# H3 mixer with token MLP on one core: the table of the last inverse stage turned by DMA transposes instead of TensorE

## The chip, the cores and the metric

One Trainium2 chip, one of its cores. The metric is the device time of one execution in microseconds (us). Engines are called by the names of the profile: PE is the matrix engine (PEld its weight loads), ACT the scalar engine, DVE the vector engine, POOL the general engine, SP the engine that mainly issues transfers. SPq stands for instructions of SP's queue that issue transfers.

## What is computed

The reference, cut to what matters (S = 2048 tokens, D = 448 channels, F = 1792; all inputs bf16):

```
x  = A_q
kv = causal_conv4(A_k, A_shift_k) * A_v                    # 4 taps along the tokens
y  = irfft(rfft(kv, 2S) * rfft(A_ssm_k, 2S))[:S]           # long convolution along the tokens
h  = x + layernorm(x) * (y + kv * A_ssm_D)
n  = layernorm(layernorm(h))
h2 = h + (gelu(n^T w1 + b1) w2 + b2)^T                     # MLP along the tokens
```

## The kernel before

**Tiles.** One SBUF tensor ("arena" in the profile) holds everything at fixed byte offsets, one PSUM tensor ("ps") has eight banks. Tokens are split as 128 partitions times R = 16 rows, so a tile is 128 x 448 bf16 for each row r.

**Stages**, each a function that appends operations under a tag. `tables` builds the tables of sines and cosines: E (32 blocks of 128 x 128 in f16; the Sin activations are tables.6:3 and tables.5:3) and the small FW, MA, MB, MN. `kT` turns the filter, `kv` does the short convolution and the product with v. `k1`, `u1` (emit_stage1) are the first forward stage of the filter and of kv: matmuls with E at L1059, evacuations at L1069 (L1067 where the D term is added), shuffles between partitions by DMA at L1075. `k2`, `u2` (emit_stage2) are the second one (matmuls L1094, evacuations L738 to L742). `i1` (emit_products_i1) multiplies the two spectra on DVE (L1160), does the first inverse stage (matmuls L1177, evacuations L738) and shuffles into TZ (L1200; the last pair in four smaller transfers, L1189). `i2` (emit_i2) is the last inverse stage: row r is two matmuls (L1299) with the blocks 2r and 2r + 1 of **ET**. ET is E with each 128 x 128 block turned. Rows 0 and 1 (r < NZ = 2) take the last pair's part from TU through EW (four more matmuls each, L1307), a small copy of ET's first blocks (transfers L1127, ct0.1:2 to 5; zeros by L1118, ct0.1:0 and 1). Then come the gate (L1316), the products, the two layernorms (statistics of x in `q`: L1236; the normalized Q at L1385) and `mlp`: first layer from W1A (L1432, weight loads L1405 called w1a.0 to w1a.3) and W1B (L1442), gelu (L1422), second layer (L1453, L1456), stores. `warm` are 14 matmuls that nobody reads (L1210), `xload` loads x in four parts (L915), `xn` normalizes x rows 0 to 3 on ACT (L1269).

**ET before.** emit_ct (L1103) is called once from i1 for the first eight blocks (step ct0.0) and once later for the other 24 (steps ct.0, ct.1, ct.2). Each step is eight PE transposes into one PSUM bank and one copy to SBUF by ACT or DVE (L738, L741).

**What sets the order.** Each engine works through its queue in order. The queues are written out in ORDER, one string per engine: a token like `i1.4:9-15` is operations 9 to 15 of step i1.4. Operations that may run on ACT or DVE are placed by the string in which they stand. Dependencies come from the byte ranges that an operation reads and writes and from `after`; the program waits on semaphores for them. shuf["u"] is the list of u1's shuffles. In i1, steps run i1.1, i1.14, i1.8, i1.10, i1.12, i1.6, i1.4, i1.16 (pairs jj = 0, 6, 3, 4, 5, 2, 1, 7); operations 18 and up of a step are its shuffles. The last queue entries of ACT before i2 are

```
i1.4:8 i1.4:17 xn.1:0 xn.2:0 i1.16:18 i1.16:9 ct.2:8 ct.0:8 xn.5:0 xn.4:0 ct.1:8
```

and SP's from the end of u1 to the first weights

```
u1.15:11 xload.2:0 xload.0:0 ct0.1:1 ct0.1:0 w1a.0:0 xload.3:0 xload.1:0 ct0.1:5 ct0.1:2-4 i1.14:20 i1.1:20 i1.1:22 ...
```

Of the kernel before, what the change touches and what calls it, by code (L numbers as in the profile page):

```python
# [13 lines left out]
        "dummy.0:1-9 kv.4:0-11 kv.3:0-7 kv.6:0-11 kv.5:0-7 kT.0:0-7 kT.1:0-7 kT.1:9 kT.3:0-7 kT.2:0-7 kT.3:9 "  # L14
        "kT.5:0-7 kT.6:0-7 kT.7:0-7 kv.7:0-7 kT.5:9 bias.0:0 k1.8:0-7 k1.9:0-2 k1.12:0-7 k1.9:3-7 kv.1:0-7 "
        "kv.2:0-11 k1.13:0-7 k1.10:0-7 k1.11:0-7 kv.8:0-3 kT.4:0-7 kv.8:4-11 kv.10:0-23 kv.12:0-23 k1.14:0-7 "
        "kv.9:0-27 k1.15:0-7 k1.4:0-7 kv.11:0-27 u1.0:0-7 u1.1:0-7 k1.0:0-7 k1.1:0-7 u1.2:0-7 u1.3:0-7 kv.13:0-27 "
        "k1.5:0-7 kv.14:0-23 k1.6:0-7 u1.4:0-7 k1.2:0-7 u1.5:0-7 kv.15:0-27 u1.6:0-7 u1.7:0-7 k1.7:0-7 u1.8:0-7 "
        "k1.3:0-7 u1.9:0-7 k2.0:0-3 k2.1:0-3 k2.12:0-3 k2.13:0-3 k2.4:0-3 k2.5:0-3 kv.16:0-23 k2.9:0-3 k2.8:0-3 "
        "u1.10:0-7 u1.12:0-7 u1.13:0-7 u1.11:0-7 u1.14:0-7 u1.15:0-7 k2.2:0-3 k2.3:0-3 k2.7:0-3 k2.6:0-3 k2.10:0-3 "  # L20
        "k2.11:0-3 k2.14:0-3 k2.15:0-3 u2.0:0-3 u2.1:0-3 u2.12:0-3 u2.13:0-3 u2.8:0-3 u2.9:0-3 u2.6:0-1 u2.7:0-3 "
        "u2.6:2-3 i1.1:1-7 i1.1:10-17 i1.1:8 i1.14:10-16 i1.14:1-7 i1.14:17 i1.14:8 i1.8:1-7 i1.8:10-16 i1.8:8 "
        "i1.8:17 ct0.0:0-7 u2.10:0-3 u2.11:0-3 i1.10:1 i1.10:10-17 i1.10:2-8 u2.5:0-3 u2.4:0-3 i1.12:1-8 "
        "i1.12:10-17 u2.2:0-3 u2.3:0-3 u2.14:0-2 i1.6:1-8 i1.6:10-17 warm.13:0 u2.14:3 u2.15:0-3 i1.4:9-15 i1.4:0-7 "
        "i1.4:16 warm.9:0 warm.11:0 warm.5:0 warm.8:0 warm.1:0 i1.16:1-7 i1.16:10-16 i1.16:8 i1.16:17 warm.10:0 "
        "warm.4:0 warm.7:0 warm.6:0 warm.0:0 ct.2:0-7 warm.12:0 warm.3:0 ct.0:0-7 ct.1:0-6 warm.2:0 i2.1:0-1 "
        "i2.2:0-3 i2.9:0 ct.1:7 i2.9:1 i2.10:0-3 i2.28:0-1 i2.45:0-1 i2.17:0-1 i2.32:0-1 i2.20:0-1 i2.41:0-1 "
        "i2.54:0-1 mlp.0:1 mlp.0:4 mlp.0:2-3 mlp.0:6 mlp.0:5 i2.58:0-1 mlp.1:2 mlp.1:4 mlp.1:3 mlp.1:5 mlp.0:0 "
        "mlp.1:1 mlp.1:6 mlp.1:0 i2.67:0-1 mlp.2:2 mlp.2:4 mlp.2:6 mlp.2:5 mlp.2:1 mlp.2:0 mlp.2:3 i2.71:0-1 "
        "mlp.3:4-5 mlp.3:2-3 mlp.3:6 mlp.3:0-1 i2.80:0-1 mlp.4:1 mlp.4:3-4 mlp.4:2 mlp.4:5-6 mlp.4:0 i2.84:0-1 "  # L30
        "mlp.5:2-3 mlp.5:0-1 mlp.5:6 mlp.5:4-5 i2.93:0-1 mlp.6:3 mlp.6:1 mlp.6:4 mlp.6:6 mlp.6:0 mlp.6:5 mlp.6:2 "
        "mlp.7:6 mlp.7:5 mlp.7:0-1 mlp.7:3-4 mlp.7:2 i2.97:0-1 mlp.8:2 mlp.8:0 mlp.8:5 mlp.8:1 mlp.8:3-4 mlp.8:6 "
        "mlp.9:5-6 mlp.9:3 mlp.9:0 mlp.9:4 mlp.9:1-2 mlp.10:5 mlp.10:3 mlp.10:2 mlp.10:6 mlp.10:4 mlp.10:0-1 "
        "mlp.11:0 mlp.11:2 mlp.11:1 mlp.11:3 mlp.11:5 mlp.11:4 mlp.11:6 mlp.12:1 mlp.12:0 mlp.12:4 mlp.12:2 "
        "mlp.12:5-6 mlp.12:3 mlp.13:6 mlp.13:2 mlp.13:1 mlp.13:3 mlp.13:0 mlp.13:4-5 mlp.14:1 mlp.14:3 mlp.14:2 "
        "mlp.14:5 mlp.14:4 mlp.14:6 mlp.14:0 mlp.15:2-3 mlp.15:5 mlp.15:1 mlp.15:6 mlp.15:4 mlp.15:0 mlp.17:0-15 "
        "mlp.18:0-15 mlp.19:0-15 mlp.20:0-15 mlp.21:0-15 mlp.22:0-15 mlp.23:0-15 mlp.24:0-13 mlp.25:0-13 "
# [15 lines left out]
    "dve": (
        "dummy.0:0 tables.3:0-1 kv.0:3 tables.6:0 tables.4:16 tables.5:0 tables.4:17 tables.6:1 tables.4:18 "
        "tables.5:1 tables.4:19 tables.6:2 tables.4:20 kv.6:12 tables.5:2 kT.1:8 kT.3:8 tables.7:6 tables.7:4 "
        "kT.5:8 kT.6:8 tables.7:7 kT.7:8 kT.0:8 bias.0:1 kv.7:8 k1.12:8 kv.2:12 kv.0:4 kT.4:8 kv.8:12 kv.10:24-25 "
        "kv.12:25 kv.12:24 kv.9:28-29 kv.11:29 kv.11:28 k1.0:8 k1.1:8 kv.13:29 kv.13:28 kv.14:25 kv.14:24 k1.2:8 "
        "kv.15:28-29 u1.7:8 k1.3:8 k2.1:5 k2.5:4 kv.16:24-25 k2.9:5 u1.10:8 u1.11:8 k2.3:4 k2.7:4 bias.1:0 k2.11:4 "
        "k2.15:5 u2.1:5 i1.0:0 i1.1:0 i1.14:0 i1.13:0 i1.7:0 i1.8:0 i1.10:0 i1.9:0 ct0.0:8 q.1:0 q.1:2 q.1:1 q.1:3 "
        "i1.11:0 q.2:0 i1.12:0 q.2:1 u2.5:5 i1.5:0 i1.6:0 i1.3:0 q.2:2 i1.2:0 q.3:0 xn.0:1 q.2:3 i1.15:0 i1.16:0 "  # L60
        "q.4:0 q.4:2-3 q.4:1 q.3:1-3 q.5:0 q.5:2-3 q.5:1 q.6:2 q.6:0-1 xn.3:1 i2.3:0 q.6:3 i2.4:0 i2.11:0 i2.5:0 "
        "i2.12:0 i2.6:0 i2.13:0 i2.18:0 i2.14:0 i2.21:0 i2.8:0 i2.16:0 i2.30:0 i2.34:0 q.7:0 q.7:2 q.7:1 q.7:3 "
        "i2.26:0 q.8:0 q.8:2 q.8:1 q.8:3 i2.27:0 i2.43:0 i2.47:0 i2.39:0 i2.40:0 i2.60:0 i2.56:0 i2.69:0 i2.52:0 "
        "i2.53:0 i2.73:0 i2.94:0 i2.82:0 i2.65:0 i2.86:0 i2.98:0 i2.66:0 i2.78:0 i2.79:0 i2.99:0 i2.95:0 i2.92:0 "
        "i2.91:0 i2.104:0 i2.105:0 mlp.24:14 mlp.25:14 mlp.26:14 mlp.27:14 mlp.28:14 mlp.29:14 mlp.30:14 mlp.31:14 "
        "mlp.32:14 mlp.33:14 mlp.34:14 mlp.35:14 mlp.36:14 mlp.37:14 mlp.38:14 mlp.39:14 mlp.39:30 "
    ),
    "pool": (
        "tables.4:0 tables.4:2 tables.4:4 tables.4:6 tables.4:8 tables.4:10 tables.4:12 tables.4:14 tables.4:1 "
        "tables.4:3 tables.4:5 tables.4:7 tables.4:9 tables.4:11 tables.4:13 tables.4:15 tables.1:0 tables.0:1-2 "  # L70
        "tables.0:0 tables.0:3-4 loads.13:0 tables.2:0-1 tables.2:3 tables.2:5 tables.2:7-11 tables.2:2 tables.2:4 "
        "tables.2:6 q.0:0-1 kv.0:1-2 tables.7:0-3 tables.7:8-11 kv.0:0 k1.9:9-10 k1.13:9-10 k1.11:9-10 k1.15:9-10 "
        "u1.1:9-10 u1.3:9-10 k1.1:9-10 k1.5:9-10 u1.5:9-10 u1.7:9-10 k1.3:9-10 k1.7:9-10 u1.9:9-10 u1.13:9-10 "
        "u1.15:9-10 u1.11:9-10 ew.0:3 ew.0:1 ew.0:0 ew.0:2 i1.14:19 i1.14:21 i1.8:19 i1.8:21 q.1:4-5 i1.10:19 "
        "i1.1:19 xn.0:0 i1.12:19 i1.6:19-20 i1.4:18 i1.6:22 q.2:4 i1.16:21 q.2:5 xn.3:0 q.4:4-5 q.6:4-5 i2.7:0 "
        "i2.15:0 i2.23:0-2 i2.24:0 i2.25:0 i2.36:0-2 i2.37:0 i2.38:0 q.8:4-5 i2.49:0-2 i2.50:0 i2.51:0 i2.62:0-2 "
        "i2.63:0 i2.64:0 i2.75:0-2 i2.76:0 i2.77:0 i2.88:0-2 i2.89:0 i2.90:0 i2.0:0 i2.101:0-2 i2.102:0 i2.103:0 "
    ),
    "sp": (
        "loads.6:0 loads.8:0 loads.0:0 loads.1:0 loads.2:0 loads.3:0 loads.13:1 loads.14:0-1 loads.10:0 loads.5:0 "  # L80
        "loads.11:0 loads.4:0-2 loads.12:0 loads.7:0 loads.9:0 k1.11:11 k1.9:11 k1.13:11 k1.15:11 u1.1:11 k1.1:11 "
        "u1.3:11 k1.5:11 u1.7:11 k1.3:11 u1.5:11 u1.9:11 k1.7:11 u1.13:11 u1.11:11 u1.15:11 xload.2:0 xload.0:0 "
        "ct0.1:1 ct0.1:0 w1a.0:0 xload.3:0 xload.1:0 ct0.1:5 ct0.1:2-4 i1.14:20 i1.1:20 i1.1:22 i1.10:21 i1.1:21 "
# [499 lines left out]
def _build(nc, A_q, A_k, A_v, A_shift_k, A_ssm_k, A_ssm_D, B_w1, B_b1, B_w2, B_b2, out):  # L583
# [14 lines left out]
    f16 = DT.float16  # L598
# [917 lines left out]
```

## Time and profile before

| what | value |
|---|---|
| three runs, us | 172.63, 172.2, 175.94 (median 172.63) |
| span of the profiled execution, us | 171.2 |
| granted clock of PE | 1.000 |
| PE busy | 161.5 us, 94% |
| DVE, ACT, POOL busy | 99.1, 92.9, 58.1 us |
| DMA packets moved | 35.15 MB, mean 205 GB/s |

The profiled execution is one execution; its own figure is the span from the first to the last instruction, 171.2 us, and no other time of it is given. The runs above are separate executions. Busy shares are means over stages with different limits: PE is near full at the end and not in the middle. In the rows of a timeline the columns are start, us from the first to the last of the merged instructions, engine, line, operation, tiles, count, and in brackets the idle time before with what ended it.

### The profile page before, as it was taken

To read this page: it belongs to the slowest core of one execution; us is meant where nothing else is said; L and a number is where in the kernel's file an instruction comes from. 1 tells how busy PE (TensorE), PEld (TensorE's weight loads), DVE (VectorE), ACT (ScalarE), POOL (GpSimd) and SP (SyncE) were. 2 spreads that over 40 slices of the span, in tenths; PEclk is the share of its full clock that TensorE was granted. 3 is DMA by queue.
4 is the path that set the end of the run, shared out by engine and by line. 5 is a ranking of instruction groups with operands and counts; after the bars stand their busy time and mean duration, and the time that the engine had idled before them with its cause. 6 is when DMAs were issued, how large, how long until landed. Compare 5 with 4: busy or idle time off the path is not lost.

```text
span 171.2 us, 3572 instructions
## 1 busy us (share of the span) xinstructions
PE 161.5 (94%) x1425; PEld 94.7 (55%) x1425; DVE 99.1 (58%) x187; ACT 92.9 (54%) x133; POOL 58.1 (34%) x150
## 2 busy tenths in 40 slices
PE   6979999979889999988999999999999999999993
PEld 2765845443334434453555555555567777777783
DVE  7988988859899999969988810000003223132232
ACT  3798788988999999999877336321210000000000
POOL 8344827590820573466788820000000000000000
PEclk9999999999999999999999999999999999999999
DMA  5999587675749855667999999960000111101111
GB/s 156 417 315 386 176 257 280 230 301 193 255 120 369 302 173 175 206 182 237 344 342 405 415 419 425 414 279 0 0 0 4 54 54 54 54 4 54 54 54 54
DMA packets 15708, 35.15 MB, mean 205 GB/s; under 512 B 3564, under 2 KB 9980, under 8 KB 15692
## 3 DMA queue, kind: packets, MB, share of 16 engines
q1 hardware_dynamic: 13020, 29.20, 46.9%
q0 software_dynamic: 2528, 5.65, 10.2%
q8 instruction: 11, 0.18, 0.5%
q10 hardware_dynamic: 144, 0.08, 0.2%
q14 instruction: 5, 0.04, 0.1%
HBM read 22.05 MB, written 1.84 MB: 139 GB/s over the span
## 4 chain that ended last, share of the span: by engine, by line
PE 66%; ACT 14%; DMA 10%; DVE 4%; POOL 2%; SPq 2%; issue 1%; DVEq 0%
PE ps L1453 25%; PE ps L1432 12%; PE ps L1442 12%; ACT arena L738 7%; DMA arena<-arena 5%; DMA arena<-in_A_ssm_k_dram 5%; ACT arena L1069 4%; PE ps L1177 4%; PE ps L1094 3%; PE ps L1299 3%; POOL arena L1075 2%; PE ps L992 2%; PE ps L1059 2%; DVE arena L1007 2%; ACT arena L739 1%
## 5 line engine op out<-in xcount | busy, mean ns | idle before, releaser
L1456 DVE SCALAR_TENSOR_TENSOR arena<-ps,arena 128x448 bf16<-128x448 f32 (+2 forms) x17 | 11.2, 657 | 57.3 <-PE ps L1453 57.2
L1453 PE MATMUL ps<-arena 128*128 128x448 bf16 (+2 forms) x238 | 42.7, 342 | 0.0
L1453 PEld LDWEIGHTS ps<-arena 128*128 128x128 bf16 x238 | 33.3, 145 | 9.5
L738 ACT CAST arena<-ps 128x896 bf16<-128x896 f32 x30 | 24.6, 1012 | 0.2 <-PE ps L1094 0.2
L1432 PE MATMUL ps<-arena 128*128 128x448 bf16 x112 | 22.5, 353 | 0.6 <-DVE arena L1385 0.6
L1069 ACT CAST arena<-ps 128x896 bf16<-128x896 f32 x24 | 20.5, 915 | 3.9 <-PE ps L1059 3.8
L1075 POOL DMA_DIRECT2D arena<-arena x32 | 17.6, 554 | 12.2 <-ACT arena L1069 10.2
L1442 PE MATMUL ps<-arena 128*128 128x448 bf16 x112 | 21.3, 352 | 0.0
L1422 ACT ACTIVATE arena<-ps,arena 128x448 bf16<-128x448 f32 x14 | 8.2, 640 | 18.7 <-PE ps L1442 14.5
L1094 PE MATMUL ps<-arena 128*64 128x448 bf16 x128 | 15.2, 359 | 2.5 <-DMA arena<-arena 0.8
L1432 PEld LDWEIGHTS ps<-arena 128*128 128x128 bf16 x112 | 10.9, 98 | 11.1 <-DVE arena L1385 1.3
L1160 DVE TENSOR_TENSOR arena<-arena 128x1792 bf16<-128x1792 bf16 x16 | 16.7, 1086 | 0.3
L1442 PEld LDWEIGHTS ps<-arena 128*128 128x128 bf16 x112 | 11.0, 98 | 10.2
L1059 PE MATMUL ps<-arena 128*32 128x448 bf16 x256 | 15.0, 355 | 0.8 <-DVE arena L1007 0.5
L1177 PE MATMUL ps<-arena 64*128 64x448 bf16 x128 | 14.5, 351 | 0.1
L1094 PEld LDWEIGHTS ps<-arena 128*64 128x64 f16 x128 | 5.8, 108 | 10.9 <-ACT arena L738 2.9
L1200 POOL DMA_DIRECT2D arena<-arena x11 | 6.5, 593 | 15.3 <-ACT arena L738 15.3
L1177 PEld LDWEIGHTS ps<-arena 64*128 64x128 f16 x128 | 6.0, 94 | 8.3 <-ACT arena L738 2.5
L1007 DVE TENSOR_TENSOR arena<-ps,arena 128x512 bf16<-128x512 f32 (+1 forms) x16 | 9.1, 619 | 2.1 <-PE ps L992 1.8
L1355 ACT ACTIVATE arena<-arena 128x448 bf16<-128x448 bf16 x14 | 8.0, 572 | 3.7 <-DVE arena L1326 3.5
L738 ACT COPY arena<-ps 128x1024 bf16<-128x1024 bf16 (+1 forms) x8 | 8.0, 1067 | 3.0 <-PE ps L966 3.0
L1059 PEld LDWEIGHTS ps<-arena 128*32 128x32 f16 x256 | 5.1, 95 | 7.6 <-DVE arena L1007 2.5
(97 smaller groups left out, 192.5 us busy)
## 6 DMA issues: line engine op xcount, KB each, us to landing
arena<-in_B_w_dram SPq DMA_DIRECT2D x8, 896.0 KB, 8.7
arena<-in_B_w_dram SPq DMA_DIRECT2D x2, 2048.0 KB, 17.3
arena<-arena POOLq DMA_DIRECT2D x32, 112.0 KB, 3.2
arena<-arena SPq DMA_DIRECT2D x16, 224.0 KB, 3.2
arena<-in_B_w_dram SPq DMA_DIRECT2D x2, 1536.0 KB, 18.8
arena<-in_A_k_dram SPq DMA_DIRECT2D x4, 448.0 KB, 5.8
arena<-in_A_v_dram SPq DMA_DIRECT2D x4, 448.0 KB, 9.4
arena<-in_A_q_dram SPq DMA_DIRECT2D x4, 448.0 KB, 5.3
```

The lines of the kernel that those rows point to most:

```text
L738: return e.copy(out=dst(), in_=src())
L1007: return e.tensor_tensor(out=v, in0=u.rearrange("p t (r d) -> p t r d", d=64), in1=v, op=ALU.mult)
L1059: op("pe", lambda e, W, b=b, r=r, q=q, x=x, c0=c0: e.matmul(PS[32 * q:32 * q + 32, b.slots[x], 0:D], E[:, 2 * r + x, c0:c0 + 32], src[:, r ...
L1069: return e.copy(out=dst, in_=Ppair(b)) if W == "act" else e.tensor_copy(out=dst, in_=Ppair(b))
L1075: shuf[tag].append(op(q_, lambda e, W, g=g, i=i, a=a, nu=nu, jh=jh: e.dma_start(T[a + i:a + i + 4 * nu - 3:4].rearrange("p (j k) c d -> p ...
L1094: op("pe", lambda e, W, b=bs[h], h=h, j=j, c=c, par=par: e.matmul(PS[64 * par:64 * par + 64, b.slots[c], 0:D], FW[:, 64 * c:64 * c + 64], ...
L1160: op("dve", lambda e, W, m=m, i=i: e.tensor_tensor(out=MR(m.slots[0]).rearrange("p (x y) d -> p x y d", x=2), in0=TU[:, i].unsqueeze(2).br ...
L1177: k = op("pe", lambda e, W, b=bs[h], m=ms[h], par=par, t=t, tab=tab, xy=xy, P=P: e.matmul(Pb(b, par), tab[P, :], MR(m.slots[0])[P, xy, :], ...
L1432: op("pe", lambda e, W, r=r, fc=fc, b=bs[fc]: e.matmul(Pb(b), W1A[:, r, 128 * fc:128 * fc + 128], Q[:, r, :], start=(r == 0), stop=(r == R ...
L1442: op("pe", lambda e, W, r=r, fc=fc, b=b: e.matmul(Pb(b), W1B[:, r, 128 * (fc - n0):128 * (fc - n0) + 128], Q[:, r, :], start=(r == 0), sto ...
L1453: op("pe", lambda e, W, r=r, fc=fc, b=b, d0=d0, d1=d1: e.matmul(Pb(b)[:, d0:d1], W2[fc // 7][:, fc % 7, r:S:R], G[:, fc, d0:d1], start=(fc ...
L1456: op("dve", lambda e, W, r=r, b=b, d0=d0, d1=d1: e.scalar_tensor_tensor(out=X[:, r, d0:d1], in0=Pb(b)[:, d0:d1], scalar=bm[:, r:r + 1], in ...
```

## The change

emit_ct issues one DMA transpose from SBUF to SBUF per group of eight blocks, on SP, after u1's shuffles. The PE transposes, their PSUM banks and the copies are gone. All queues of ORDER are written anew, of which the lines below show the parts around the change.

```diff
         def emit_ct(late):
             for h in range(1, 4) if late else range(1):
                 sch.t0 = T_CT + 0.1 * h
-                b = _Buf(psum)
-                for i in range(8):
-                    op("pe", lambda e, W, b=b, h=h, i=i: e.transpose(
-                        out=Pbf(b, 0, f16)[:, 128 * i:128 * i + 128], in_=E[:, 8 * h + i, :], identity=IH),
-                       r=[(o_E + 2048 * h + 256 * i, 256), (o_IH, 256)], bw=[b], kind="tr", safter=i1_last[-1:])
-                evac(lambda h=h: ET[:, 8 * h:8 * h + 8, :].rearrange("p a b -> p (a b)"),
-                     lambda b=b: Pbf(b, 0, f16), [(o_ET + 2048 * h, 2048)], b, 1024,
-                     est={"act": 904.0, "dve": 600.0})
+                op("sp", lambda e, W, h=h: e.dma_start_transpose(
+                    out=ET[:, 8 * h:8 * h + 8, :], in_=E[:, 8 * h:8 * h + 8, :].rearrange("p a b -> p (a b)")),
+                   r=[(o_E + 2048 * h, 2048)], w=[(o_ET + 2048 * h, 2048)], dmab=128 * 2048, est=700.0, rate=400.0,
+                   after=shuf["u"])
```

The queues after, in parts ("..." where entries are left out):

```
pe   ... k1.4:0-7 u1.2:0-7 k1.0:0-7 k1.5:0-7 u1.3:0-7 k1.1:0-7 u1.4:0-7 kv.14:0-23 kv.15:0-27 kv.13:0-27 k1.6:0-7
     k1.2:0-7 u1.5:0-7 u1.6:0-7 k1.3:0-7 k1.7:0-7 u1.7:0-7 u1.8:0-7 u1.9:0-7 k2.0:0-3 ...
     i1.4:9-15 i1.4:0-5 i1.4:16 i1.4:6-7 warm.13:0 warm.8:0 warm.0:0 i1.16:1-8 i1.16:10-17 warm.5:0
     warm.10:0 warm.9:0 warm.7:0 i2.1:0-1 i2.2:0-3 i2.9:0-1 i2.10:0-3 i2.32:0 i2.45:0-1 i2.41:0-1 i2.17:0-1
     i2.54:0-1 i2.20:0-1 i2.28:0 warm.12:0 i2.28:1 i2.58:0-1 i2.32:1 mlp.0:1 ...
act  kv.4:12 tables.6:3 kT.1:8 kT.0:8 kT.3:8 kT.5:8 kv.7:8 k1.8:8 bias.0:1 k1.12:8 k1.9:8 kv.1:8 k1.10:8 k1.11:8
     tables.5:3 k1.15:8 u1.0:8 u1.1:8 u1.2:8 k1.5:8 u1.3:8 tables.0:5 u1.4:8 tables.7:5 ...
     i1.4:17 i1.4:8 i1.16:9 i1.16:18 xn.1:0 xn.4:0 xn.5:0 xn.2:0 i2.46:0 ...
dve  ... i1.10:0 i1.9:0 q.1:0 q.2:2 q.2:0 q.1:2 i1.12:0 i1.11:0 ... i1.15:0 q.6:0 i1.16:0 ...
     i2.3:0 q.6:3 i2.4:0 i2.11:0 i2.5:0 i2.6:0 i2.12:0 i2.18:0 i2.13:0 i2.14:0 i2.8:0 i2.21:0 i2.59:0 i2.16:0 ...
sp   ... u1.15:11 ct.1:0 ct0.1:1 ct0.1:0 xload.0:0 ct0.0:0 xload.1:0 ct.0:0 xload.3:0 ct0.1:3 xload.2:0 ct.2:0
     i1.1:20 i1.1:22 ct0.1:4 i1.1:21 i1.10:21 i1.12:21 ct0.1:2 i1.14:20 i1.6:21 ct0.1:5 i1.4:20 i1.16:19-20
     i1.16:22 i1.12:22 w1a.0:0 i1.10:22 i1.4:19 i1.8:20 w1a.1:0 w1a.2:0 ...
```

In these, tables.0:5 is a Sin activation of one element that stood first in ACT's queue before; tables.5:3 and tables.7:5 are further Sin activations. Operation 8 of a k1 or u1 step is its evacuation. On DVE, i2.4 and i2.12 are statistics of rows 0 and 1, i2.6 a step of row 0's variance, i2.8 row 0 of Q, i2.21 the product of row 3. Before, their order was i2.5, i2.12, i2.6, ..., i2.21, i2.8.

## The prediction

> **What bounds the kernel now.** I read the stages first (busy time by stretch), then the chain of waits, then the timelines of ACT, PE and SP where the edit sits. The stretches (us of PE, PEld, DVE, ACT, POOL with instruction counts, clock, DMA share, GB/s):
>
> ```profile
> 13.50:35.00 21.50, 20.07 (x433) 11.86 (x432) 18.56 (x27) 17.69 (x22) 12.99 (x25) 1.00 0.74 254
> 48.00:70.70 22.70, 21.82 (x192) 9.04 (x190) 22.44 (x31) 22.70 (x29) 7.54 (x14) 1.00 0.68 223
> 75.20:104.90 29.70, 29.07 (x154) 14.91 (x155) 20.40 (x63) 19.82 (x45) 18.87 (x43) 1.00 0.95 351
> 104.90:168.20 63.30, 63.30 (x347) 43.72 (x345) 10.26 (x15) 7.37 (x13) 0.00 (x0) 1.00 0.22 89
> ```
>
> From 48 to 70.7 ACT is full: 22.70 of 22.70 us, evacuations without a hole. From 75.2 on PE is all but full (its 29.07 lacks 0.63, below), and from 104.9 it has no hole at all. So the end is set by when the last inverse stage (L1299) starts plus the holes of PE behind it. The chain around that start:
>
> ```profile
> 70.72 1.25 ACT arena L1269 x2
> 71.96 0.81 ACT arena L738
> 73.06 2.14 DMA arena<-arena
> 75.20 0.53 PE ps L1299 x2
> 80.58 0.32 DVE arena L1385
> 80.95 1.31 PE ps L1432 x6
> ```
>
> The chain names the 98 KB transfer issued at 73.06. I don't follow it there: rows 0 and 1 of i2 read nothing of that transfer (r < NZ takes the last pair from TU through EW), and the transfer that POOL issued at 71.01 (i1.4:18, 196 KB) has a landing time of 4.1 in the DMA view of that stretch, so 75.1. That is the wait that ends at 75.19. The pair issued from 72.8 on is needed 12 matmuls later, at about 77.5. PE and ACT in the same place:
>
> ```profile
> 72.48 0.61 PE L1108 MATMUL ps<-arena 128*128 128x128 f16 x8
> 75.19 0.54 PE L1299 MATMUL ps<-arena 128*128 128x448 bf16 x2 [0.69 <-DMA arena<-arena]
> 80.95 1.31 PE L1432 MATMUL ps<-arena 128*128 128x448 bf16 x6 [0.63 <-DVE arena L1385]
> ```
>
> ```profile
> 73.29 2.11 ACT L738 COPY arena<-ps 128x1024 f16<-128x1024 f16 x2
> ```
>
> **Part by part.** Removed on PE: 32 transposes. Eight (ct0.0) lie in the ACT-full stage; at 0.055 us spacing (0.61 less the 0.22 of the last, over 7) that is 0.44 us. They cost nothing because ACT ends later; without that cover they would be worth 0.44. Of the other 24, 23 fill PE while it waits for the DMA that lands at 75.1: nothing. One stands among the i2 matmuls: **-0.06 us**.
>
> Removed on ACT: three copies (2.11 + 1.01 us) behind the last i1 evacuation; ACT's next bound work is the gate at 78.09, which waits for PE. Nothing. Removed on DVE: one copy of 0.69 us at 57.35. DVE's order takes two bn_stats (0.53 each in effect) in its place, so i1.16's product comes some 0.4 us later than at 70.3. It feeds the last pair, whose data have slack up to 77.5: nothing.
>
> Moved on ACT: the two xn activations (1.25 us in the chain) go behind i1.16's evacuations. By the chain that is 1.25 us gained; by my reading it is nothing, because i1.4's transfer ends the wait and i1.4's evacuations stay the 27th and 28th of 28 at 0.81 us. Bounds -1.25 and 0, taken 0.
>
> The hole before the MLP: 0.63 us, DVE's Q row 0 comes late. New order: i2.6 ahead of i2.12 (bn_stats, 0.55 us) and i2.8 ahead of i2.21 (0.6 us), and three more i2 matmuls at 0.19 plus a filler stand before mlp.0. Bounds -0.63 and 0, taken **-0.5 us**.
>
> Moved on SP: w1a.0, from 51.69 to behind i1.16's three transfers and i1.12:22. These end at 74.98 now; the pair's evacuations are some 0.8 us earlier without xn, and one transfer of 0.72 comes on top, so w1a.0 goes out at about 74.9. It is needed at 80.4. The four loads of that line land 4.8 (min), 6.4 (median), 11.0 us (max, behind the others) after issue. At 4.8: 79.7, nothing. At 6.4: 81.3, so +0.9. At the 8.7 that all eight loads of 896 KB have as median: 83.6, so +3.2. Row nearest: w1a.1, issued at 76.99 among the same transfers, 4.8. Taken 0.
>
> Early stage, 13.5 to 35: DVE takes three more evacuations net (1.05 each) and 1.3 us of table work that ran before 13.5, plus 0.4 of a copy, and gives 0.85: 18.56 becomes about 22.5 us in a stretch of 21.5. ACT becomes about 19.2. Against it, k2 starts at 35.04 after 0.83 us of waiting for shuffles, and one more u1 group than now separates the last k1 from it. Bounds: -0.83, and +2.9 if DVE keeps its present idle time as well. The two pull opposite ways; taken 0. POOL takes over four table operations (2.20 + 1.01 us) between the shuffles that it issues; it is busy for 12.99 of 21.5, so they fit, and k2's first half has the slack of one more group. The Sin dummy leaves the head of ACT's queue, so the table load (1.28 us at 0.72) comes before the first real Sin. That Sin starts at 8.19 now; its input is ready near 6.3 in the new order, so 6.4 + 1.28 = 7.7: covered; without cover +1.28.
>
> Added: **four DMA transposes** of 256 KB on SP. The SP queue (start, us, count):
>
> ```profile
> 49.20 0.81 SPq L915 DMA_DIRECT2D arena<-in_A_q_dram  x2
> 50.05 1.59 SPq L1118 DMA_DIRECT2D arena<-arena  x2
> 52.17 0.97 SPq L915 DMA_DIRECT2D arena<-in_A_q_dram  x2
> 58.06 2.70 SPq L1127 DMA_DIRECT2D arena<-arena  x4
> 60.80 10.61 SPq L1200 DMA_DIRECT2D arena<-arena  x8
> ```
>
> All four wait for u1's last shuffles, as the x loads do now (49.20), and everything behind them on SP waits: the x loads (bn_stats on DVE, in order ahead of the i1 products; x0 is needed at 57.4), the EW fills, i1's shuffles. ct0.1:3 is a new wait: it reads what ct0.0 writes and holds x2, ct.2 and the shuffles behind it; two x loads and a transpose stand between, some 3 us, about the time in which such a transfer lands (4.2). Let each hold SP for T. Ahead of i1.4:20 then stand 1.59 + 1.78 (x loads) + 0.67 (one fill) + 10 issues at 0.72 = 11.2 us plus 4T, from 49.2: 60.4 + 4T. i1.4:20 goes out at about 70.7 now, so it is late from **T = 2.6 us** on. No row shows a transposing DMA. Lower bound of T: a plain issue, 0.43. Upper: SP held until a transfer between 196 KB (4.2 us) and 448 KB (5.3 us) has landed, 4.5. At the 254 GB/s of the busy stage above, 256 KB move in 1.0 us, so I take T = 1.5: covered by 4.3 us of SP slack. Their 1.05 MB take 4 us of the 16 queues, against 2.3 us that w1a.0 leaves there.
>
> The Trainium skill ("Advanced Engine Details and Errata", X-Bar Transpose) says that such transposes run as fast as plain DMAs, 350 to 400 GB/s. By that figure, an estimate, the four would move in 2.8 us and the sum stays.
>
> **Sum:** -0.06 - 0.5 = -0.56 us on a span of 171.2. The median of the runs is 172.63, 1.4 us above that span, and I keep the 1.4: 172.1.
>
> **Rivals.**
> *SP is held (slower).* T above 2.6: i1.4:20, and with it the start of i2, is late by 4(T - 2.6). From T = 3.5 on the kernel is more than 2% slower; at 3.8 it is +4.8 - 0.06, so 177.4; at 4.5, 180. For it: a transposing transfer may have to drain what stands before it (three of four follow an x load). Against: no plain issue holds SP over 0.82 us.
> *Block by block (slower).* A 128x128 block is 32 KB, and the 32 KB store has a landing time of 1.5 us. Eight such trips one after the other are T = 12: +37.6, 210. No row speaks for it.
> The Trainium skill ("VectorE: DVE Perf Modes", The three transpose paths) gives 1309 ns for one 128x128 block through DMA and advises TensorE; as an estimate, 32 of them are 41.9 us.
> *PE cools.* Without 24 transposes and with only four fillers after i1.16, PE stands idle from about 72.4 to 75.2, 2.8 us. The first nine matmuls of the kernel took 3.19 us, 0.35 each, against 0.19 for the same shape later: a cold PE is half as fast for some 3.2 us. Price 1.6: 173.7. Against: the present holes (0.83, 0.81) show no such thing, but they are short.
> The Trainium skill ("TensorE: Matmul & The Clock Gate", Part 1) puts the fall after an idle window of about 3.4 us; by that rule 2.8 us is just too short.
> *Early stage or w1a.0 late.* +2.9 or +3.2 less 0.5 kept: 174.5 to 175.3, and with both over 176.
> *All that is covered counts (faster).* -0.44 - 1.25 - 0.63 - 0.83 - 0.06 = -3.2, plus the 0.28 hole of ACT there: 169.1.
>
> **Chances.** Forecast 0.40 (its own range 170.5 to 173.8). PE cools 0.14. SP held 0.21, block by block 0.03. Early stage or w1a.0 0.12, a quarter of it over 2%. All counts 0.10. A measurement of this kernel tells about 2% from no change, 3.5 us. Faster: 0.10. Slower: 0.21 + 0.03 + 0.03 = 0.27. Same: 0.63. The range from 169.2 to 178.5 leaves out half of the last case and half of the SP cases, 0.17.
>
> **What would show it.** In the profile after: SP issues of the new transposes, each below 2.6 us from start to the next issue; i1.4:20 at about 70.7; L1299 starting between 74.4 and 75.6 after a wait for DMA; no hole before L1432; the i2 matmuls at 0.19 us spacing; 28 evacuations on ACT without a hole. Wrong if L1299 starts after 77, if L1432 waits for in_B_w_dram, or if k2 (L1094) starts after 36.

## The result, and the profile after

The changed kernel takes 180.03 us (median of 4 runs, 178.91 to 180.69), the kernel before 172.58 us beside it: ratio 1.0408, 95% interval 1.0336 to 1.048. By the ratio it is slower by 7.0 us; 172.1 us was forecast. In all comparisons below the ratio is the number to read: it leaves out executions far above the fastest of the same kernel, of which the kernels with DMA transposes had several (one lay at 183.94 us where its fastest took 173.77), the kernels without them few.

The profiled execution took 180.28 us, its span is 178.5 us against 171.2. The same view by stretches as before, cut where the stages of the changed kernel end (us of PE, PEld, DVE, ACT, POOL with counts, clock, DMA share, GB/s):

```profile
13.50:35.00 21.50, 20.85 (x441) 11.86 (x439) 20.15 (x32) 18.96 (x23) 13.42 (x29) 1.00 0.76 260
48.00:70.70 22.70, 21.85 (x185) 9.10 (x185) 22.41 (x31) 22.48 (x29) 10.56 (x16) 1.00 0.89 202
70.70:80.70 10.00, 2.74 (x21) 0.93 (x20) 6.39 (x18) 5.76 (x8) 5.84 (x10) 0.83 0.90 247
80.70:110.00 29.30, 29.06 (x143) 13.93 (x144) 19.28 (x60) 16.69 (x39) 17.64 (x42) 0.94 0.98 360
```

Three things to see. From 48 to 70.7 ACT is as full as it was (22.48 of 22.70), but the DMA engines went from a share of 0.68 to 0.89 while they move less (202 GB/s, not 223). From 70.7 to 80.7 PE works 2.74 us of 10 and none of the other four engines is full, while the DMA engines have a share of 0.90: everybody waits for transfers. And the clock of PE is below 1 in the last two rows, where it was 1.00.

The chain of waits around the start of the last inverse stage:

```profile
66.57 0.60 POOL arena L1201
67.19 0.81 POOL arena L1245
68.01 1.51 POOL arena L1248
69.52 0.59 POOL arena L1201
70.19 1.02 POOL arena L1248
71.21 1.00 POOL arena L1257
72.21 1.13 POOL arena L1201 x2
73.34 7.31 DMA arena<-arena
80.74 0.90 PE ps L1300 x2
81.64 1.49 PE ps L1308 x4
```

L1201 are the shuffles of i1, L1245 to L1257 small operations of the statistics of q and of xn. On POOL they now stand ahead of i1.4:18, the transfer that ends the wait for i2. It goes out at 73.34 instead of 71.01 and lands 7.3 us later instead of 4.1. i2 starts at 80.74 instead of 75.19. When its data were ready is seen on ACT, where the last two evacuations of each of these rows are those of i1.4 (before, then after):

```profile
63.20 7.51 ACT L738 CAST arena<-ps 128x896 bf16<-128x896 f32 x9
63.66 8.28 ACT L743 CAST arena<-ps 128x896 bf16<-128x896 f32 x10
```

They end at 70.71 and 71.94. So of the 5.55 us by which i2 starts later, 1.23 lie ahead of the data, 1.1 between the data and the issue (1.40 us instead of 0.30, POOL's queue), and 3.2 in the landing.

The groups of PE behind it show the clock as well (busy us, mean ns of one, idle before):

```profile
L1300 PE MATMUL ps<-arena 128*128 128x448 bf16 x32 | 8.9, 380 | 6.8 <-DMA arena<-arena 6.7
L1308 PE MATMUL ps<-arena 128*128 128x448 bf16 x8 | 2.8, 491 | 0.0
L1433 PE MATMUL ps<-arena 128*128 128x448 bf16 x112 | 22.5, 353 | 0.1
```

L1299 and L1307 of before (now L1300 and L1308) had 352 ns each and 0.7 us of idle time. In the chain above four matmuls take 1.49 us, 0.37 each, where a warm PE starts one every 0.19.

The transposes themselves, in the timeline of SP's queue (start, us, count):

```profile
50.37 1.35 SPq L1111 DMA_TRANSPOSE arena<-arena  x1
53.92 2.10 SPq L1111 DMA_TRANSPOSE arena<-arena  x1
56.68 1.23 SPq L1111 DMA_TRANSPOSE arena<-arena  x1
59.89 1.26 SPq L1111 DMA_TRANSPOSE arena<-arena  x1
```

### The profile page after: what moved, and what is told of

The parts are those of the page before. It is cut to its first block, busy times and chain, and to the rows that moved or that the text cites. A ratio compares the mean times of both kernels' runs of the same rounds, so it can differ in the third digit from the quotient of the medians.

```text
span 178.5 us, 3521 instructions
## 1 busy us (share of the span) xinstructions
PE 162.0 (91%) x1393; PEld 92.6 (52%) x1393; DVE 99.8 (56%) x186; ACT 91.5 (51%) x131; POOL 61.2 (34%) x150
## 4 chain that ended last, share of the span: by engine, by line
PE 58%; ACT 16%; POOL 9%; DMA 9%; DVE 5%; issue 2%; ACTq 0%; POOLq 0%; DVEq 0%
PE ps L1454 24%; PE ps L1443 12%; ACT arena L743 11%; PE ps L1433 10%; DMA arena<-arena 9%; POOL arena L1080 3%; PE ps L1300 2%; DVE arena L747 2%; PE ps L1099 2%; PE ps L1030 2%; POOL arena L1248 1%; PE ps L1308 1%; POOL arena L1201 1%; PE ps L1064 1%; ACT arena L852 1%
## 5 line engine op out<-in xcount | busy, mean ns | idle before, releaser
L743 ACT CAST arena<-ps 128x896 bf16<-128x896 f32 (+1 forms) x31 | 24.8, 969 | 0.6 <-DVE arena L1161 0.3
L1433 PE MATMUL ps<-arena 128*128 128x448 bf16 x112 | 22.5, 353 | 0.1
L1443 PE MATMUL ps<-arena 128*128 128x448 bf16 x112 | 21.3, 352 | 0.0
L1074 ACT CAST arena<-ps 128x896 bf16<-128x896 f32 x21 | 18.0, 910 | 3.0 <-PE ps L1064 1.8
L1433 PEld LDWEIGHTS ps<-arena 128*128 128x128 bf16 x112 | 10.8, 98 | 10.7 <-DVE arena L1386 1.2
L1300 PE MATMUL ps<-arena 128*128 128x448 bf16 x32 | 8.9, 380 | 6.8 <-DMA arena<-arena 6.7
L1317 ACT ACTIVATE arena<-ps,arena 128x448 f32<-128x448 f32 x10 | 7.1, 720 | 9.1 <-PE ps L1300 8.5
L1201 POOL DMA_DIRECT2D arena<-arena x11 | 6.6, 606 | 12.0 <-ACT arena L743 12.0
```

The costliest lines, as they stand in the source:

```text
L743: return e.copy(out=dst(), in_=src())
L1074: return e.copy(out=dst, in_=Ppair(b)) if W == "act" else e.tensor_copy(out=dst, in_=Ppair(b))
L1300: k = op("pe", lambda e, W, b=b, r=r, h=h: e.matmul(Pb(b), ET[:, 2 * r + h, :], TZ[:, r, h, :], start=(h == 0), stop=(h == 1 and r >= NZ)) ...
L1433: op("pe", lambda e, W, r=r, fc=fc, b=bs[fc]: e.matmul(Pb(b), W1A[:, r, 128 * fc:128 * fc + 128], Q[:, r, :], start=(r == 0), stop=(r == R ...
L1443: op("pe", lambda e, W, r=r, fc=fc, b=b: e.matmul(Pb(b), W1B[:, r, 128 * (fc - n0):128 * (fc - n0) + 128], Q[:, r, :], start=(r == 0), sto ...
```

## The experiments

Theory 1: the new order costs the time, the transposes are cheap. Theory 2: the transposes clog the DMA engines. Theory 3: the cold clock is a price of its own. The table gives all that ran (i2: start of the last inverse stage in the profile; gap: idle time of PE just ahead of it; rest: from i2's start to the end of the span; for e13 and e14 the three were not read). For e4 no ratio came out; its four executions took 175.81 to 183.55 us, the profiled one 175.81.

| kernel | ratio to before (95%) | i2 | gap | rest |
|---|---|---|---|---|
| before | 1 | 75.19 | 0.7 | 96.0 |
| changed | 1.0408 (1.0336 to 1.048) | 80.74 | 6.7 | 97.8 |
| e1 old order, DMA transposes | 1.0284 (1.0198 to 1.0371) | 77.82 | 3.9 | 98.5 |
| e2 new order, PE transposes | 1.0309 (1.023 to 1.0389) | 79.17 | 3.3 | 97.5 |
| e3 changed, POOL's queue mended | 1.0441 (1.0375 to 1.0507) | 79.46 | 5.3 | 98.4 |
| e4 changed, early stage of before | none | 76.19 | 4.0 | 97.8 |
| e5 changed, 26 more warm matmuls | 1.0263 (1.0208 to 1.0317) | 79.27 | 0.3 | 96.1 |
| e6 e1, 16 more warm matmuls | 1.0217 (1.0133 to 1.0301) | 79.50 | 3.6 | 96.1 |
| e7 e1, copies for transposes | 1.0182 (1.0132 to 1.0231) | 76.17 | 2.9 | 97.5 |
| e8 e1, transposes at 37 to 49 us | 1.0044 (1.002 to 1.0067) | 74.93 | 1.6 | 96.1 |
| e9 e2, POOL's queue mended | 1.0182 (1.0137 to 1.0228) | 76.97 | 1.3 | 96.5 |
| e10 e9, early stage of before | 1.0104 (1.0061 to 1.0146) | 75.62 | 1.0 | 97.0 |
| e11 e8, transposes spread from 29 us | 1.0549 (1.0485 to 1.0613) | 81.97 | 3.0 | 97.6 |
| e12 changed, transposes at 38 to 51 us | 1.076 (1.0695 to 1.0825) | 85.12 | 4.9 | 98.9 |
| e13 e3 and 18 more warm matmuls | 1.028 (1.0212 to 1.0347) | | | |
| e14 e13, early stage of before | 1.011 (1.0055 to 1.0166) | | | |
| e15 e8, two transposes put back | 1.0123 (1.0061 to 1.0185) | 76.41 | 1.5 | 96.1 |
| e16 e1, w1a.0 moved late | 1.0084 (1.0021 to 1.0146) | 74.79 | 1.7 | 97.6 |

### Each half alone: e1 and e2

e1 is the old order with the four DMA transposes in SP's queue; the PE transposes and their copies are dropped from the other queues:

```diff
-u1.15:11 xload.2:0 xload.0:0 ct0.1:1 ct0.1:0 w1a.0:0 xload.3:0 xload.1:0 ct0.1:5 ct0.1:2-4 i1.14:20
+u1.15:11 xload.2:0 xload.0:0 ct0.1:1 ct0.1:0 ct0.0:0 w1a.0:0 xload.3:0 ct.0:0 xload.1:0 ct.1:0 ct0.1:5 ct0.1:2-4 ct.2:0 i1.14:20
```

> The order of before, with the four DMA transposes put into SP's queue (the first behind the zero fills of the EW route, the others among the x loads and the first shuffles), the 32 TensorE transposes and their four evacuations gone, nothing else moved. Theory 1 (the new order costs, the transposes are cheap: each held SP 1.2 to 2.1 us in the changed kernel): 171 to 174 us, i2 starting within 1.5 us of the 75.2 us of before. Theory 2 (the transposes' packets clog the DMA queues, so that x loads and shuffles land late): 177 to 180 us, i2 starting at 79 us or later.

e2 is the new order with emit_ct of before: `ct0.0:0-7` behind `i1.8:8`, `ct.2:0-7 ct.0:0-7 ct.1:0-7` behind `warm.7:0` on PE, their copies on DVE and ACT, and no `ct` transposes on SP.

> The order of the changed kernel, with the 32 TensorE transposes and their four evacuations put back where before has them (one behind the fourth pair of i1, three behind the warm matmuls ahead of i2) and no DMA transpose. Theory 1 (order): 177 to 181 us, i2 starting at 79 us or later. Theory 2 (transposes): 172 to 174.5 us, i2 starting at 75 to 77 us.

Both theories got their slow half and neither its fast one (though e1's i2 started sooner than the 79 us named for it): either half alone costs most of the whole, 2.8% and 3.1%, and together they cost 4.1%. So they share something. One shared thing is in the table: each has a gap of over 3 us ahead of i2, and a rest of 97.5 or 98.5 us instead of 96.0.

### The clock: e5 and e6

e5 adds 26 warm matmuls, e6 adds 16, on PE just ahead of i2 (`warm.14:0` to `warm.39:0` behind `warm.7:0`, N_WZ raised; in e6 behind `warm.2:0`).

> The changed kernel with 26 further warm matmuls on TensorE between the last of its warm matmuls and i2, at 0.19 us each some 4.9 us of the 6.7 us for which TensorE stood idle there; nothing else changed. The clock's theory (the gap lets the granted clock fall, and i2 and the start of the MLP run at 0.37 us a matmul instead of 0.19): i2 still starts near 80.7 us, its matmuls stay 0.19 us apart, the mean granted clock is 1.000, and the time 178 to 178.6 us, 1.5 to 2.2 us under the changed kernel. Its rival (what comes behind i2's start is bound by the evacuations and the normalisation, and TensorE's clock is hidden): 179.5 to 180.5 us with the clock at 1.000.

> The order of before with the four DMA transposes, as in the first experiment, with 16 further warm matmuls ahead of i2 (3.0 us of the 3.9 us for which TensorE stood idle there). The clock's theory: of the 5.1 us that this kernel's profiled span was over the span of before, 2.0 to 2.5 us came after i2's start and go away, the other 2.6 us stay: 175.3 to 176.3 us, clock 1.000. Its rival (the late landings alone count): 177.5 to 178.5 us.

The PE groups of e5:

```profile
L1303 PE MATMUL ps<-arena 128*128 128x448 bf16 x32 | 8.2, 353 | 0.4 <-PE ps L1214 0.3
L1311 PE MATMUL ps<-arena 128*128 128x448 bf16 x8 | 1.8, 352 | 0.0
```

i2's matmuls are at 353 ns again, the clock is 1.000, and the rest is 96.1 us, as in before. e5 gains 1.45 points on the changed kernel, 2.5 us, somewhat more than expected (177.53 us against 178 to 178.6; its i2 also started 1.5 us sooner: i1.4:18 went out at 73.37 and landed 5.7 us later instead of 7.3, and nothing in the edit explains that). In e6 the rest falls from 98.5 to 96.1 us, but its i2 happened to start 1.7 us later than e1's; the ratios of e1 and e6 overlap. By the rests the cold clock is worth 1.6 us of 7.0 (changed kernel against e5) to 2.4 us of 4.9 (e1 against e6), a quarter to a half of the loss. The rest alone does not tell a cold clock, though: e16 has 97.6 us at a clock of 1.00, for another reason (below).

When the clock falls can be read in the traces. The half clock lasted 3.41 us (e2, e4, e7) or twice that (the changed kernel, e1, e3), and ahead of the fall all six had run at full clock for 71.68 us, 21 times 3.41. So it is set for stretches of 3.41 us, which do not start where a gap starts. Here are the stretch that ends with the fall in e7 and the one behind it, then the two that hold the gap of e6 (columns as above, the third from the end is the clock):

```profile
74.00:77.41 3.41, 1.25 (x7) 0.71 (x8) 1.17 (x4) 1.41 (x2) 1.96 (x4) 1.00 0.68 221
77.41:80.83 3.42, 3.42 (x11) 1.32 (x9) 2.52 (x6) 0.42 (x1) 1.28 (x2) 0.50 0.39 82
74.35:77.76 3.41, 1.60 (x9) 0.61 (x7) 0.50 (x3) 1.41 (x2) 1.36 (x3) 1.00 0.65 234
77.76:81.17 3.41, 1.67 (x9) 0.90 (x10) 0.32 (x1) 0.00 (x0) 0.00 (x0) 1.00 0.49 176
```

PE was idle for 2.2 us of the stretch in e7, and the next one ran at half clock. In e6 the longer gap, 3.6 us, is split into 1.8 and 1.7, and the clock held. In all traces the stretch ahead of a fall has 1.88 us (e11) or more of idle time, and none that kept the clock has more than 1.82 (e6).

### The order: e3, e9, e4 and e10

The mend of POOL's queue, in e3 with the DMA transposes and in e9 with those on PE:

```diff
-ew.0:0 tables.7:10 i1.8:21 ew.0:3 i1.14:19 ew.0:2 i1.14:21 i1.8:19 q.2:4 i1.10:19 ew.0:1 i1.12:19 q.1:4
-q.2:5 i1.6:19 q.1:5 xn.3:0 i1.1:19 i1.6:22 i1.4:18 i1.6:20 q.4:4 xn.0:0 i1.16:21 q.4:5
+ew.0:0 tables.7:10 ew.0:3 ew.0:2 ew.0:1 i1.14:19 i1.14:21 i1.8:19 i1.8:21 i1.1:19 q.2:4 i1.10:19 i1.12:19
+q.1:4 i1.6:19 i1.6:20 q.2:5 i1.4:18 i1.6:22 q.1:5 xn.3:0 i1.16:21 q.4:4 xn.0:0 q.4:5
```

> The changed kernel with one stretch of POOL's queue mended: the seventh pair's first transfers ahead of the one of the fourth pair that waits longer, the first pair's transfer right behind them, and three of the statistics operations behind the transfer of the second pair. Theory 1: the late transfer of the second pair goes out at 72.2 us or sooner instead of 73.3 us, and lands some 4 us later instead of 7.3 us, with fewer transfers just ahead of it: i2 starts at 76 to 77.5 us, and the time is 174.5 to 177 us. Theory 2: the landing stays slow, 7 us behind the issue, and the time at 178.5 to 180.5 us.

> The second experiment (order of the changed kernel, transposes on TensorE) with POOL's queue mended as in the third. If POOL's queue is what the new order costs once the DMA engines are not full: i2 starts at 76 to 77.5 us instead of 79.2, and the time is 173.5 to 176 us. Rival (the late products of the early stage and the vector engine's order set it, as the chain of the third experiment read): i2 at 78 us or later and 177 to 179 us.

With the transposes on PE the mend is worth 1.3 points (2.2 us; the intervals of e2 and e9 do not overlap). These are POOL's shuffles in e2 and in e9; i1.4:18 is the third of the four in e2, at 73.90, and the first in e9:

```profile
72.72 2.32 POOL L1205 DMA_DIRECT2D arena<-arena  x4
72.52 1.19 POOL L1205 DMA_DIRECT2D arena<-arena  x2 [1.01 <-ACT arena L743]
```

i2 starts at 76.97 instead of 79.17. With the DMA transposes the mend shows no gain. The chain of e3 shows why:

```profile
74.24 0.40 SPq L1201
74.68 0.65 SPq L1128
75.37 4.04 DMA arena<-arena
79.46 0.93 PE ps L1300 x2
```

The wait moved to SP. L1128 is the last of the copies that bring rows 0 and 1 of i2 through EW; in e3 it goes out at 74.68, because SP's queue was held further up:

```profile
59.79 4.99 SPq L1111 DMA_TRANSPOSE arena<-arena  x1
64.82 2.47 SPq L1201 DMA_DIRECT2D arena<-arena  x2
67.33 2.14 SPq L1128 DMA_DIRECT2D arena<-arena  x1
```

With POOL's shuffles out sooner, the fourth transpose holds SP for 4.99 us (1.26 in the changed kernel). That the one causes the other is not shown.

e4 and e10 put the old order of everything up to the end of k2 into the changed kernel and into e9 (each engine's queue: the entries of dummy, tables, loads, kv, kT, bias, k1, u1 and k2 as in before, then the others as they were).

> The changed kernel with everything up to the end of k2 on all five engines in the order of before (tables, loads, kernel transforms, stage 1 of k and u with its shuffles), and everything from u2 on in the order of the changed kernel. Theory 1 (the new early order costs the 1.23 us by which u2's evacuations start later): u2 starts 1.2 us sooner, and the end with it, 178 to 179.3 us. Theory 2 (what counts is the slow landing ahead of i2, and the early delay is hidden behind it): 179.5 to 180.5 us.

> The kernel of the ninth experiment with everything up to the end of k2 in the order of before as well; what is left of the new order are u2, i1, the x loads, the shuffles on SP, the late load of the first quarter of the weights and the MLP. If the early order costs its 0.8 to 1.2 us: that much less than the ninth experiment, 172.3 to 174.5 us, i2 starting at 75 to 76.5 us. Rival (the late half of the order costs all of it): within 0.5 us of the ninth.

e10 is 0.8 points under e9, 1.35 us, as the early delay read in the profile (u2's evacuations start at 49.17 instead of 47.94 in the changed kernel); the intervals overlap slightly, and the start of i2 moves by the same 1.35 us. e4's i2 started at 76.19, more than the 1.2 us sooner that either theory gave, so its landings were sooner too; without a ratio it shows no more. What is left in e10, 1.0 point or 1.8 us, is the late half of the new order. It was not taken apart. Its last product on DVE starts at 70.39 where before has 69.33, behind four bn_stats that were put ahead of the ninth product instead of two, and PE then waits 0.46 us within i2 for a transfer of that last pair; that is read, not tried. A part of this is the hybrid's own: e10 has the copy of ct0.0 on DVE again (0.69 us), which the changed kernel has not.

### The traffic: e7, e8 and e16

How busy the DMA engines are between 48 and 78 us, in the DMA view: packets first, then SP's hardware queue (packets, MB, share of 16 engines). Before:

```profile
DMA packets 3334, 6.31 MB, mean 210 GB/s; under 512 B 864, under 2 KB 2416, under 8 KB 3332
q1 hardware_dynamic: 2296, 4.28, 41.9%
```

e1:

```profile
DMA packets 7450, 7.25 MB, mean 242 GB/s; under 512 B 5042, under 2 KB 6536, under 8 KB 7448
q1 hardware_dynamic: 6443, 5.25, 65.4%
```

The four transposes add 4178 small packets and 23.5 points of 30 us: by this difference 7.0 us of all sixteen engines, 1.76 us for each 256 KB, or 149 GB/s. The share of all queues goes from 0.65 to 0.90. Alone a transpose takes less. The first one of the changed kernel moves beside only 32 other packets; its DMA view from 51.5 to 52.9 us:

```profile
DMA packets 1056, 0.26 MB, mean 187 GB/s; under 512 B 1056, under 2 KB 1056, under 8 KB 1056
q1 hardware_dynamic: 1056, 0.26, 83.0%
```

83.0% of 1.4 us are 1.16 us of all sixteen engines, 226 GB/s. So a third of the 7.0 us comes only where the engines have other work as well. Is it this traffic, or the hold of SP's queue? e7 replaces each transpose by a plain copy of 256 KB in pieces of 256 bytes:

```diff
-op("sp", lambda e, W, h=h: e.dma_start_transpose(
-    out=ET[:, 8 * h:8 * h + 8, :], in_=E[:, 8 * h:8 * h + 8, :].rearrange("p a b -> p (a b)")),
+op("sp", lambda e, W, h=h: e.dma_start(
+    out=ET[:, 8 * h:8 * h + 8, :], in_=E[:, 16 * (h // 2) + h % 2:16 * (h // 2) + 16:2, :]),
```

> The first experiment with each DMA transpose replaced by a plain DMA copy of the same 256 KB from SBUF to SBUF in pieces of 256 bytes, issued at the same place of SP's queue; the table of i2 is not transposed, so the values of the output are left out of account. Traffic theory (1024 pieces of 256 bytes each take the 16 DMA engines some 1.6 us a transpose, and the shuffles behind them land later for it): DMA packets under 512 bytes near 5,000 between 48 and 78 us as with the transposes, i2 starting at 77 us or later, 176 to 178.5 us. Hold theory (what costs is that a transpose holds SP's queue 1.4 to 3.3 us, where a plain issue holds it 0.5 to 0.8): the shuffles behind them go out 4 us sooner, i2 starts at 75 to 76 us, 172 to 174 us.

The queue of e7 in the same stretch:

```profile
q1 hardware_dynamic: 6451, 5.32, 61.0%
```

It falls between: 1.8% over before, 3.1 us, against 4.9 us with transposes; the two intervals overlap. By the same difference the pieces alone take 5.7 of the 7.0 us of engine time, and some two thirds of the loss, while the copies held SP for only 0.60 to 1.47 us each (1.36 to 3.27 in e1). Hold and traffic are hard to part, either way: in e7 a plain issue behind the copies occupied SP for 3.62 us (L1122 at 56.60, else 0.7).

e8 keeps the transposes and moves them to where the engines stood idle; they no longer wait for u's shuffles (`after=shuf["u"]` is dropped):

```diff
-... k1.7:11 u1.13:11 u1.11:11 u1.15:11 xload.2:0 ... ct0.0:0 ... ct.0:0 ... ct.1:0 ... ct.2:0 ...
+... k1.7:11 ct.1:0 ct.2:0 u1.13:11 u1.11:11 u1.15:11 ct0.0:0 ct.0:0 xload.2:0 ...
```

> The first experiment with the four DMA transposes at other places of SP's queue and no longer behind the shuffles of u: two right behind the last shuffle issue of k (near 38 us) and two behind the last shuffle issue of u (near 44.5 us), where the trace shows the DMA engines idle (40.5 to 42.5 us and 45.5 to 48.5 us). Traffic theory: their 1.6 us each falls into idle time, the stretch from 48 to 78 us is again as busy as before (65 percent), i2 starts at 75 to 76.3 us and the time is 172 to 174 us. Its rival (the shuffles of u wait behind them, so that k2 and u2 start later): u2 starts 1 us or more later, and the time is 174 to 177 us.

The chain of e8 ahead of i2:

```profile
71.14 0.58 POOL arena L1194
71.74 3.18 DMA arena<-arena
74.93 0.54 PE ps L1293 x2
```

The transfer lands 3.2 us after its issue and i2 starts at 74.93, a little sooner than in before. The loss shrinks from 4.9 to 0.8 us (1.0044), with the same transposes, holds of 2.05 to 2.71 us each and the same order elsewhere. The place was the cost.

e16 leaves them in place and moves w1a.0, 896 KB, out of the stretch, behind the last pair's shuffles (`i1.16:19 w1a.0:0 i1.8:22`), where the new order has it.

> The first experiment (order of before, DMA transposes in place) with the load of the first quarter of the weights (896 KB, w1a.0) moved behind the last pair's shuffles, where the changed kernel has it; nothing else moved. Traffic theory: the four transposes (some 6.5 us of all 16 DMA engines) then stand in a stretch that lost some 2.2 us of bulk load, the shuffles of i1 land sooner, i2 starts at 75 to 77 us, and the time is 173.5 to 176 us. Rival (a transpose holds back what moves beside it, and the weight load has no part in that): 177 to 179 us as the first experiment.

It takes 2 of the 2.8 points away, and i2 starts at 74.79, a little sooner than in before, with all four transposes in place. What is left lies behind i2's start: PE's first matmuls of the MLP, and the DMA view from 74.9 to 75.4 us, in which w1a.0 is issued (size, us to landing):

```profile
82.09 1.30 PE L1427 MATMUL ps<-arena 128*128 128x448 bf16 x6 [2.10 <-DVE arena L1321]
arena<-in_B_w_dram SPq DMA_DIRECT2D x1, 896.0 KB, 7.0
```

Issued at 74.92, the weights land at 81.9, and PE, idle for 2.10 us, goes on at 82.09. The row of Q that these matmuls read is done at 80.8 (L1380), so it is the late weights that they wait for; the DVE operation that the row names only ended at about that time.

The new order has w1a.0 late too, which may be why the transposes add less to it (e2 to the changed kernel: 1.0 point, 1.7 us, with overlapping intervals) than to the old (2.8). The engines' share is 0.91 in e16 as well, so the share alone doesn't tell e1 and e16 apart.

### Other places: e11, e12 and e15

e11 is e8 with one transpose in each of four places (`k1.5:11 ct.1:0 u1.7:11`, `k1.7:11 ct.2:0`, `u1.15:11 ct.0:0`, `xload.1:0 ct0.0:0`), e12 the changed kernel with e8's places (`k1.3:11 ct.1:0 ct.2:0`, `u1.15:11 ct0.0:0 ct.0:0`), e15 e8 with two of them behind the x loads and the EW copies.

> The eighth experiment with the four DMA transposes spread further: one in the gap of SP's queue at 29 us, one behind the last shuffle issue of k, one behind the last of u, one behind the last x load (all in the order of before, so that each falls into idle time of the DMA engines or ahead of a gap of SP's queue). Traffic theory: u2 starts as in before, nothing is late ahead of i2, and the time is 172.0 to 173.2 us, between the eighth experiment and before; a version that beats before by more than 0.3 us is not expected, since i2's start in before waits for a shuffle and not for the TensorE transposes. Rival (a transpose slows whatever moves beside it, wherever it stands): 173.5 to 175 us.

> The changed kernel with only its four DMA transposes moved, to the places of the eighth experiment (two behind the last shuffle issue of k, two behind the last of u). If the two costs are separate: the transposes' share goes, the order's share stays, and the time is that of the second experiment, 176.5 to 179 us. If the new order is harmless once the DMA engines are free: 172.5 to 175 us. If the transposes' place does not matter in this order, because POOL's queue sets i2's start: 179.5 to 180.5 us.

> The eighth experiment with two of the four DMA transposes moved back behind the x loads and the copies of the EW route (near 53.5 and 57 us, ahead of a gap of the DMA engines), one left behind the last shuffle issue of k and one behind the last of u. Traffic theory: the shuffles of u go out 0.7 us sooner than in the eighth experiment, and the DMA engines are idle at 57 to 60 us: 172.3 to 173.8 us, within 0.5 percent of before. Rival (a transpose behind 50 us delays the shuffles of i1, wherever it stands): 174.5 to 177 us.

e11 and e12 missed every theory by far: 1.0549 and 1.076. The chain of e11:

```profile
29.78 8.45 DMA arena<-arena
38.27 4.27 PE ps L1093 x24
```

The transpose issued at 28.58 stands among the shuffles for which k2 waits; they land 8.45 us after the last issue, and k2 starts at 38.27 instead of 35.04. The one behind u's shuffles does it again: the first x load goes out at 55.37 instead of 49.20. In e12 the pair at 37.84 and 39.72 meets five shuffles that POOL sends out at 38.05 to 40.19 in the new order (the last one is out at 37.98 in the old); the one at 38.59 lands after 7.53 us. A stretch that is idle in one order is not idle in another. e15, 1.2%, lies between e8 and e1, as two of four would; by the ratio these are 174.9 us, in the range of the rival. No place tried beats before, and none of the runs points to a version that would.

### The sum: e13 and e14

> The third experiment (changed kernel, POOL's queue mended) with 18 further warm matmuls ahead of i2, 3.4 us of the 5.4 us for which TensorE stood idle there. If the clock hid what the mended queue gained: clock 1.000, i2 starting at 78.5 to 79.8 us, 175 to 177 us, that is 0.5 to 2.5 us under the fifth experiment. Rival (with the DMA engines 88 percent busy the landings are late whatever POOL's queue does): 177 to 178.5 us, as the fifth.

> The thirteenth experiment with everything up to the end of k2 in the order of before. If the costs add up: 1.2 us under the thirteenth, 174 to 176 us; against the tenth experiment (the same order with the transposes on TensorE, 174.5 us) what is then left over is the traffic of the transposes in place, 0 to 2 us. Rival (traffic in place is worth the 2.6 us and more of the first experiment here too): 177 us or more.

e13 (e3 and 18 warm matmuls) lies at 2.8%, beside e5's 2.6%: with DMA transposes the mend of POOL's queue shows no gain, as its rival said. e14 adds the old early stage and comes to 1.1%, the level of e10, but its four executions took 174.22 to 184.23 us, so it shows little. That spread is not explained.

One path from before to the changed kernel, by ratios: late order 1.8 us (e10), early order 1.35 (e9), POOL's queue 2.2 (e2), transposes in the new order 1.7; together 7.05 us, with the clock's 1.6 to 2.4 us inside these. That the steps add up proves nothing, since each is the difference of two neighbours on the path. Another path shares the loss out differently: in the old order the transposes cost 4.9 us (e1), and with DMA transposes the mend of POOL's queue gains nothing (e3). Each step carries 0.7 to 1.9 us of uncertainty, and the interval of the last one takes in 0.

## Why the prediction was wrong, point by point

- **Where the bound sits: right.** The end is set by i2's start and what PE loses behind it; 5.55 of the 7.3 us of span are i2's later start, 1.75 the rest.
- **i2's start: the step that failed.** The transfer named, i1.4:18, is the one that ends the wait. But its time was left at 71.01 plus 4.1 us, and it was 73.34 plus 7.3. The part "moved" walked SP's and ACT's new order and POOL's early table operations; it did not walk POOL's queue up to this transfer, and the rule that a queue runs in order was applied to SP alone. In the profile this is 1.1 us of the issue; by e2 and e9, with the transposes on PE, it is worth 2.2 us. And the landing was kept at 4.1 us although 1.05 MB were added to the same stretch: 3.2 us.
- **Traffic of the transposes: seen, mis-sized and left out of the sum.** The four were put at 4 us of the 16 queues. At the 1.16 us of one alone they would take 4.6, near enough; beside the traffic of the old order they added 7.0. What failed is that only the hold of SP was given a price: in the old order the same traffic costs 4.9 us in place and 0.8 elsewhere.
- **T: right in this profile, wrong as a constant.** Taken 1.5, measured 1.23 to 2.10, all below the 2.6 from which it would count; i1.4:20 went out at 71.97, as soon as ACT had its data. But a hold was 3.84 in e6 and 4.99 in e3, the latter beyond the upper bound of 4.5. The rival "SP is held" took place in e3, where the EW copy was late by it. What makes a hold long is not shown.
- **PE cools: a rival at 0.14 that came true.** Its gap was put at 2.8 us; it was 6.7, because i2 came later. Its price of 1.6 us measured 1.6 to 2.4, in part by luck: it was worked out for 3.2 us at half clock, which lasted 6.83 us here, of which PE worked 3.33.
- **Early stage: taken 0, measured 1.35 us** (e9 to e10), inside its bounds. The sign set for it showed: k2 starts at 36.40, after 36. The first Sin, said to be covered, starts at 8.72 instead of 8.19, as its table is loaded only at 7.43, behind a copy; this was not tried by itself.
- **The hole ahead of the MLP: right, worth little.** L1433 has 0.1 us of idle time, not 0.63, and did not wait for the weights. w1a.0 went out at 76.22, not 74.9, and landed 9.2 us later, at 85.4, without harm, as i2 itself was late. In e16 the rival "w1a.0 late" came true.
- **The copies taken from ACT and DVE: nothing, as said.** e8, without them, starts i2 at 74.93.
- **Block by block: no.** The four landed 4.7 us (median) after their issue. All that is covered counts: no.
- **Sums.** The upper bound of the early stage, worded as DVE keeping its idle time, would be the whole added work, 4.0 us, and not 2.9, which is that idle time. With 2.9 and the 0.5 kept its rival would start at 175.0 us, not 174.5. Half of the last case and half of the SP cases are 0.155, not 0.17, and 0.185 with block by block. None of this moves the forecast of 172.1.

The Trainium skill ("Advanced Engine Details and Errata", X-Bar Transpose) gives 350 to 400 GB/s for such transposes; the 226 GB/s of one alone and the 149 beside other traffic do not agree, and the measurement decides. The Trainium skill's rule for the clock ("TensorE: Matmul & The Clock Gate", Part 1) lets the clock fall after an idle window of some 3.4 us that is free-running. The traces agree on the free-running window, the stretches of 3.41 us above; they do not agree that it must be idle as a whole, since 1.88 us of idle time in it were enough (e11).

## What to carry to other kernels

Price a transfer that is added in time of the DMA engines as well as in time of the queue that issues it, and look for what stands behind it on both, since the same four transposes cost 4.9 us in one place and 0.8 us in another. When an order is searched anew, walk every in-order queue up to the transfer that ends the critical wait, the engine that seems idle first. A gap of TensorE of some 2 us or more can be paid twice, once as the gap and once, about 2 us, as a cold clock; the warm matmuls of e5 and e6 kept the clock at 1.000.

## What the runs showed of the hardware

- A DMA transpose of 256 KB from SBUF to SBUF is about 1024 packets of 256 bytes. Alone it took 1.16 us of all sixteen DMA engines, beside other traffic 1.76 us, and a plain copy in the same pieces there 1.4 us (7.0 and 5.7 for four). Its issue held SP between 1.23 and 4.99 us.
- Beside this traffic plain issues hold the queue too: 3.62 us for a 4 KB copy in e7, 2.33 and 2.08 us for single shuffles in e5 and e6, against 0.67 in before.
- The length of PE's gap does not decide alone: the clock fell with a gap of 2.9 us (e7) and held with one of 3.6 us (e6). It is set for stretches of 3.41 us by PE's idle time in the one before: 1.88 us or more let it fall, up to 1.82 kept it. In e7 it fell 1.2 us after PE had resumed.
- Kernels with DMA transposes in a busy stretch vary by up to 10 us between executions (e16, 173.77 to 183.94), the one with plain copies of the same pieces by 0.8 us (e7, 175.37 to 176.16, four executions). Whether the transposing does this, and how, stays open.
